# Channel attention and two feed-forward layers: a running account of engine time sets where weight and data operations stand

## The chip, the cores and the metric

The kernel runs on one core of a Trainium2 chip. The metric is the device time of one execution in microseconds (us). Below, PE is TensorE (matmuls; PEld is its weight load), ACT is ScalarE, DVE is VectorE, POOL is GpSimd and SP is SyncE, which here only issues DMAs.

## What is computed

```python
qn = q / (norm(q, axis=tokens) + 1e-6);  kn = k / (norm(k, axis=tokens) + 1e-6)
a = softmax(kn.T @ qn / tau)                  # 256 x 256, over 6080 tokens
x = v @ a                                     # 6080 x 256
x = square(relu(x @ w_in_1)) @ w_out_1        # 256 -> 2048 -> 256
h = x @ w_in_2                                # 256 -> 2048
y = (h * clip(h + 3, 0, 6) / 6) @ w_out_2     # 2048 -> 256
```

All inputs are float32 except the four weight matrices, which come as float64 words and are turned into float32 on the chip.

## The kernel before

**Steps.** After a head (scores, softmax, first weights) the program is a list of 96 steps, numbered i = 0 to 95 as in the code. There are two layers (`ph` 0 and 1), six chunks of tokens per layer (`c`), four blocks of 512 hidden columns (`u`) and two halves of such a block (`p`); a chunk is thus 8 steps. Every matmul product is made of three fp32r matmuls (high times high, high times low, low times high), and the 2 x 2 block products are done in seven multiplications, M1 to M7, instead of eight (Strassen's scheme in Winograd's form). A step (`step`, L764) runs the seven multiplications of its own hidden columns, 21 matmuls, and between them the 24 output matmuls of the step before, 45 in all. From step 8 on TensorE's order in a step is: M1, M2, M5, 3 output matmuls, M6, 5 outputs, M7, 6 outputs, M4, 5 outputs, M3, 5 outputs. So M6 is matmul 12 of the step, M7 matmul 20, M4 matmul 29 and M3 matmul 37, counted from 0.

**What TensorE waits for.** M1, M6, M7 and M4 share one PSUM tile `x`. After M1 ScalarE copies it out as `m1`, after M6 as `u2`, after M7 as `u3`, and after M4 it takes the activation of it (`act_psum`, tile `r`). M6 may start only when the copy `m1` has read the tile, M7 when `u2` has, M4 when `u3` has; M3 may start when VectorE has added `h22 = u3 + y`. VectorE makes the four sums h11, h22, h21 (here ScalarE and VectorE share), h12, and their activations (L806 in layer 0); ScalarE then rounds each to the high operand (`g<-h`), and VectorE subtracts to get the low operand (`g<-h,g`). What is left of h12 at the end of a step, its activation and its two operands, is done in the next step (`carry`).

**Background work.** The second layer's weights are prepared during the first layer's chunks 1 to 5, in tasks (`add_in_2`, `add_out_2`). For each `u` there are two conversions of `w_in_2` (`conv(0)`, `conv(1)`), each six operations: ScalarE `ct<-w` and `cv<-w`, then VectorE `ct<-ct` (L126), `ct<-ct` (L130), `ct<-ct,cv` (L142) and `wblk<-w,ct` (L134). A third task (`part`) takes from both conversions' blocks `wblk`: ScalarE rounds to a staging tile (`st<-wblk`, L108), VectorE subtracts (`st<-wblk,st`), SP stores both to DRAM. `w_out_2` goes the same way in two tasks (`convert_split`). Beside the tasks there is a `lane` of operations that split the next chunk's data (`b<-blk` on ScalarE; `blk<-blk` and `b<-blk,b` on VectorE). ScalarE, VectorE, SP, POOL and TensorE each work through their own queue in order; from step 8 on (`MANUAL_FROM = 8`, `phase[0] = 2`) these queues stand exactly in the order in which the source emits them.

**Where it is put.** `quota(i)` says how many background operations a step must take, `lane_quota(i)` the same for the lane. `beside(at)`, called at seven fixed places of the step, takes fixed shares of the two (`BESIDE_2`, `LANE`) and emits them there; an operation marked `waits` ends such a batch early.

```python
def beside(at):
    parts = BESIDE if i < MANUAL_FROM else BESIDE_2
    k = -(-todo[0] * parts[at] // max(1, sum(parts[at:])))
```

Of the kernel before, what the change touches and what calls it, by code (L numbers as in the profile page):

```python
# [62 lines left out]
def tile_channel_attention_then_two_ffn(  # L63
# [89 lines left out]

    def weight_sums(r):
        a21, a22, a11, a12 = (r[:, i] for i in range(4))
        return [
            lambda: add(a22, a21, a22),
            lambda: sub(a21, a11, a21),
            lambda: sub(a11, a22, a11),
            lambda: sub(a12, a12, a11),  # L160
        ]

    def data_prep(r, n, slots, new):


        b12, b22, b11, b21 = (r[:, i, :n] for i in range(4))
        of = {0: b22, 1: b11, 2: b21, "b12": b12, 3: b12, 4: b22, 5: b11, 6: b21}

        def one(slot):
            if slot == "sums":  # L170
                return [lambda: sub(b11, b12, b11), lambda: sub(b12, b22, b12),
                        lambda: sub(b22, b22, b11), lambda: sub(b21, b21, b22)]
# [5 lines left out]
            return [hi, lambda: sub(t[0][:, 1, :n], of[slot], t[0][:, 0, :n].bitcast(F32))]  # L178
        return [f for slot in slots for f in one(slot)]

    RAW, OTHER, SUMS = ((0, 3),), ((3, 4),), ((3, 5), (5, 7))
# [5 lines left out]
    def split_slots(r, ops, cuts):  # L187

        def one(a, b):
            parts = []  # L190

            def hi():
                parts.extend(t[:, a:b] for t in ops())
                return copy_act(parts[0], source(r, a, b))
            return [hi, lambda: sub(parts[1], source(r, a, b), parts[0].bitcast(F32))]
        return [f for cut in cuts for f in one(*cut)]

    def new_ops(pool, name):
# [13 lines left out]
    class Task:  # L212
        def __init__(self, name, load, due, alone, size):
            self.name, self.load, self.due, self.alone, self.size = name, load, due, alone, size
            self.steps, self.since = None, 0
# [18 lines left out]
    last_lo = [None, None, None]  # L234
    held, gate, marks = [], [], {}

    def waits(f):
        f.waits = True
        return f

    def background(n=1, calm=False):
        first = True
        while n > 0 and tasks:
            turn[0] ^= 1
# [3 lines left out]
            if calm and not first and getattr(t.steps[0], "waits", False):  # L248
                break
            first = False  # L250
            with ExitStack() as behind:
                for ins in gate if phase[0] == 1 else ():
                    behind.enter_context(tc.issue_after(ins))
                if t.name in held:
                    behind.enter_context(tc.issue_after(last_lo[2]))
                if phase[0] == 1:
                    for ins in marks.get(HELD_BEHIND.get(t.name), []) + marks.get("now", []):
                        behind.enter_context(tc.issue_after(ins))
                t.steps.pop(0)()
            n -= 1  # L260
            done[0] += 1
            if not t.steps:
                finished.add(tasks.pop(k).name)
                turn[0] = 0
                ensure_loads()
        return n

    def front(n, k=0):

# [33 lines left out]
    def out_cut(w, u, a):  # L303
        return w[u * 512 + a * P:u * 512 + (a + 2) * P]

    def convert_split(w, n, parts, done=None, fine=False, mark=True):

        def load():
            ws = words(w, n)
            got, x = [], []  # L310

            def make():
                steps, dst = from_f64_steps(None, ws, fine)
                x.append(dst)
                return steps

            def hi():
                got.extend(parts())
# [10 lines left out]
            return late(make, 6 if fine else 3) + [waits(hi), waits(lo)]  # L329
        return load  # L330

    def late(make, n):

        got = []

        def at(i):
# [4 lines left out]
            return waits(f) if i == n // 3 else f  # L341
        return [at(i) for i in range(n)]

    for u in range(NU):
        pool, tag = (gp, "g") if u == 0 else (oop, "oh")
# [6 lines left out]
    def add_w1(u, due=0, halves=(0, 1)):  # L352
        def conv(h):
            fine = u == 1 or (u, h) == (0, 1)

            def load():
                ws = words(in_cut(w_in_1, u, h), 1)
                return late(lambda: from_f64_steps(w1[u][:, h:h + 1], ws, fine)[0], 6 if fine else 3)
# [26 lines left out]
    def add_in_2(u, due):  # L385
# [3 lines left out]
        def conv(h):  # L389
            def load():  # L390
                ws = [x[:, 0].rearrange("p (g f) -> p g f", g=2) for x in words(in_cut(w_in_2, u, h), 1)]

                def make():
                    if not r:
                        r.append(blocks_tile("wblk"))
                    return from_f64_steps(r[0][:, h:4:2], ws, FINE)[0]
                return late(make, 6 if FINE else 3)
# [17 lines left out]
    def add_out_2(u, due):  # L415
        kept["o", u] = [dram.tile([P, 4, C], F32, tag="o2" + t, name="o2" + t, bufs=NU) for t in "hl"]
        for a in (0, 2):
            add_task(("o2", u) if a else None,
                     convert_split(out_cut(w_out_2, u, a), 2, lambda: staged(2),
                                   lambda st, a=a: keep([d[:, a:a + 2] for d in kept["o", u]], st), FINE), due)  # L420

    def fetch_2(nm, u):
        need((nm + "2", u))
# [279 lines left out]


    y_ps = {}

    def out_mms(ph, c, u, p, g):

# [24 lines left out]
    def y_done(ph, c, b, e, last=False):  # L733
# [15 lines left out]
        for k, (i, j) in enumerate(zip(cuts, cuts[1:])):  # L749
            if k:  # L750
                DVE.tensor_scalar(out=t[:, i:j], in0=y[:, i:j], scalar1=scale, scalar2=None, op0=ALU.mult)
            else:
                ACT.activation(out=t[:, i:j], in_=y[:, i:j], func=AF.Copy, scale=scale)
            (nc.gpsimd if ph == 0 else ACT if last and not k else SP).dma_start(out=dst[:, i:j], in_=t[:, i:j])

    def run_outs(outs, n):
        for _ in range(min(n, len(outs))):
            f, done = outs.pop(0)
            f()
            if done:  # L760
                y_done(*done)

    def step(i, ph, c, u, p, before, outs, carry):
# [2 lines left out]
        n = chunks[c][1]  # L766
        wh, wl = w_ops[ph, u]
        b_slots = b_ops[ph, c]
        todo = [quota(i) * (1 if i <= LAST else (0, 2)[i % (LAST + 1)] if i % (LAST + 1) < 2 else 1)]
        lane_todo = [lane_quota(i)]  # L770
        nxt_lane = bool(lane)

        def mul(dst, m, first):
# [2 lines left out]
            hi, lo = (b_slots[b][:, x, :n] for x in range(2))  # L776
            for k, (w, x) in enumerate(((wh, hi), (wh, lo), (wl, hi))):
                PE.matmul(dst, w[:, a, rows], x, start=first and k == 0, stop=k == 2, skip_group_check=True)  # L778

        def pop(k):  # L780
            run_outs(outs, k)

        def beside(at):
            parts = BESIDE if i < MANUAL_FROM else BESIDE_2
            k = -(-todo[0] * parts[at] // max(1, sum(parts[at:])))
            todo[0] -= k
            if k:
                todo[0] += background(k, phase[0] == 2)
# [58 lines left out]
        if plain:  # L847
# [27 lines left out]
            pop(len(outs))  # L875
            return g, (lambda: relu2(h12, x, 3), hi12, lo12)

        x = bank()[:, :n]
        mul(x, M1, True)
        marks["now"] = [copy_act(m1, x).ins]  # L880
        run(before)
        carry[0]()
        carry[1]()
        beside(0)
        pp = bank()[:, :n]
        mul(pp, M2, True)
# [1 line left out]
        carry[2]()  # L888
        y = bank()[:, :n]
        mul(y, M5, True)  # L890
        pops = AW_POPS if i == 0 else POPS if i < MANUAL_FROM else POPS_2
        pop(pops[0])
        act(h11, "1")
        beside(1)
# [163 lines left out]
```

## Time and profile before

| | us |
|---|---|
| time, median of 3 runs (lowest to highest) | 1072.03 (1071.76 to 1072.09) |
| the profiled execution, its own time | 1071.73 |
| its span, first to last instruction | 1069.9 |
| TensorE busy in the span | 1061.6 |
| VectorE, ScalarE, POOL busy | 896.7, 650.6, 22.5 |

The profiled execution has 1.8 us outside the span. Matmuls overlap in the records: one lasts some 0.39 us, but the next begins 0.23 us after it. A busy share of 99% therefore does not say that nothing is lost; the distance between the starts of neighbouring matmuls does.

### The profile page before, as it was taken

How to read it: one execution, taken by the hardware profiler on the slowest of the kernel's cores; microseconds unless marked ns; L12 is line 12 of the kernel's file. 1: busy time of each engine (PE TensorE's matmuls, PEld its weight loads, DVE VectorE, ACT ScalarE, POOL GpSimd, SP SyncE). 2: the span in 40 equal slices, each digit the busy share in tenths (PEclk: the TensorE clock that was granted, in tenths of full speed). 3: DMA queues.
4: the chain of work that ended last, by engine and by line, in shares of the span. 5: the costliest groups of instructions: out<-in, count | busy, mean ns of one | idle time of the engine just before them, and what ended most of it. 6: DMA issues, size and time to landing. Idle time of an engine off the chain costs nothing.

```text
span 1069.9 us, 12845 instructions
## 1 busy us (share of the span) xinstructions
PE 1061.6 (99%) x4602; PEld 865.6 (81%) x4602; DVE 896.7 (84%) x1520; ACT 650.6 (61%) x1129; POOL 22.5 (2%) x46
## 2 busy tenths in 40 slices
PE   9999999999999999999999999999999999999998
PEld 8778887888888888788888888888888888888886
DVE  6999888978878787887878988898898898898785
ACT  6698886566666667566565455455545555555443
POOL 0000000000000000001101000000000000000000
PEclk9999999999999999999999999999999999999999
DMA  9632230033123121314545002002002001001001
GB/s 359 246 99 91 67 118 20 30 121 95 40 95 102 50 68 69 108 46 174 181 152 185 1 1 78 1 1 78 1 1 78 1 1 59 20 0 39 1 1 39
DMA packets 31648, 78.03 MB, mean 73 GB/s; under 512 B 3296, under 2 KB 13792, under 8 KB 31584
## 3 DMA queue, kind: packets, MB, share of 16 engines
q1 hardware_dynamic: 27024, 57.49, 16.1%
q0 software_dynamic: 3840, 17.76, 4.8%
q10 hardware_dynamic: 720, 1.96, 0.5%
q8 instruction: 36, 0.59, 0.2%
q14 instruction: 28, 0.23, 0.1%
HBM read 53.22 MB, written 23.99 MB: 72 GB/s over the span
## 4 chain that ended last, share of the span: by engine, by line
PE 96%; DVE 2%; ACT 1%; DMA 0%; issue 0%; SPq 0%; ACTq 0%; DVEq 0%
PE y L720 48%; PE s L778 43%; PE sc L569 4%; PE s L499 1%; DMA w<-w_out_dram 0%; PE s L534 0%; DVE b L111 0%; ACT g L108 0%; DVE h L806 0%; DVE h L114 0%; DVE wl L111 0%; DVE g L111 0%; ACT ct L138 0%; ACT u L108 0%; DVE ct L142 0%
## 5 line engine op out<-in xcount | busy, mean ns | idle before, releaser
L720 PE MATMUL y<-g,oh 128*128 128x506 f32 (+1 forms) x1536 | 508.7, 392 | 0.0
L778 PE MATMUL s<-b,wh 128*128 128x506 f32 (+1 forms) x1356 | 422.4, 393 | 2.6 <-ACT u L108 1.9
L111 DVE TENSOR_TENSOR g<-h,g 128x506 fp32r<-128x506 f32 (+1 forms) x384 | 262.3, 683 | 99.4 <-ACT g L108 80.5
L720 PEld LDWEIGHTS y<-g,oh 128*128 128x128 f32 x1536 | 289.3, 188 | 64.4 <-DVE g L111 0.4
L778 PEld LDWEIGHTS s<-b,wh 128*128 128x128 f32 x1356 | 254.4, 188 | 63.7 <-ACT u L108 4.3
L720 PE MATMUL y<-g,ol 128*128 128x506 f32 (+1 forms) x768 | 302.0, 393 | 0.0
L778 PE MATMUL s<-b,wl 128*128 128x506 f32 (+1 forms) x678 | 266.0, 392 | 0.2 <-DVE wl L111 0.2
L108 ACT ACTIVATE g<-h 128x506 fp32r<-128x506 f32 (+1 forms) x384 | 235.3, 622 | 36.3 <-DVE h L827 14.2
L108 ACT ACTIVATE u<-s 128x506 f32<-128x506 f32 (+1 forms) x180 | 107.0, 595 | 141.7 <-PE s L778 140.7
L720 PEld LDWEIGHTS y<-g,ol 128*128 128x128 f32 x768 | 144.6, 188 | 31.8
L778 PEld LDWEIGHTS s<-b,wl 128*128 128x128 f32 x678 | 127.9, 189 | 29.0 <-DVE wl L111 1.1
L114 DVE TENSOR_TENSOR h<-u,s 128x506 f32<-128x506 f32 (+1 forms) x180 | 122.1, 678 | 27.2 <-ACT u L108 26.2
L108 ACT ACTIVATE m<-s 128x506 f32<-128x506 f32 (+1 forms) x90 | 53.6, 596 | 105.9 <-PE s L778 105.2
L810 DVE SCALAR_TENSOR_TENSOR h<-r,h 128x506 f32<-128x506 f32 (+1 forms) x144 | 98.9, 687 | 4.9
L806 DVE SCALAR_TENSOR_TENSOR h<-h 128x506 f32<-128x506 f32 (+1 forms) x121 | 82.6, 683 | 1.4
L826 ACT ACTIVATE r<-s,three 128x506 f32<-128x506 f32 (+1 forms) x48 | 32.9, 686 | 59.7 <-PE s L778 59.7
L114 DVE TENSOR_TENSOR h<-m,s 128x506 f32<-128x506 f32 (+1 forms) x90 | 61.2, 680 | 6.7 <-PE s L778 3.2
L809 DVE TENSOR_SCALAR r<-h 128x506 f32<-128x506 f32 (+1 forms) x144 | 60.6, 421 | 1.7
L111 DVE TENSOR_TENSOR b<-blk,b 128x506 fp32r<-128x506 f32 (+1 forms) x85 | 57.6, 680 | 0.9 <-ACT b L108 0.9
L108 ACT ACTIVATE b<-blk 128x506 fp32r<-128x506 f32 (+1 forms) x85 | 52.1, 616 | 0.2 <-DVE blk L111 0.2
L823 ACT ACTIVATE r<-s 128x506 f32<-128x506 f32 (+1 forms) x42 | 24.9, 594 | 32.5 <-PE s L778 30.0
L827 DVE SCALAR_TENSOR_TENSOR h<-r,s 128x506 f32<-128x506 f32 (+1 forms) x48 | 32.7, 681 | 9.7 <-ACT r L826 9.7
(97 smaller groups left out, 525.8 us busy)
## 6 DMA issues: line engine op xcount, KB each, us to landing
w<-w_in_dram SPq DMA_DIRECT2D x16, 512.0 KB, 4.6
w<-w_out_dram SPq DMA_DIRECT2D x16, 512.0 KB, 3.8
k<-k_dram SPq DMA_DIRECT2D x10, 512.0 KB, 7.0
blk<-vT_dram SPq DMA_DIRECT2D x8, 506.0 KB, 4.3
y<-y POOLq DMA_DIRECT2D x16, 253.0 KB, 2.5
blk<-y SPq DMA_DIRECT2D x8, 506.0 KB, 4.9
outT_dram<-y SPq DMA_DIRECT2D x15, 253.0 KB, 2.1
q<-q_dram SPq DMA_DIRECT2D x7, 512.0 KB, 7.7
```

Source lines behind the costliest of these rows:

```text
L108: return ACT.activation(out=out, in_=in_, func=AF.Copy)
L111: return DVE.tensor_tensor(out=out, in0=a, in1=b, op=ALU.subtract)
L114: return DVE.tensor_tensor(out=out, in0=a, in1=b, op=ALU.add)
L569: return lambda: PE.matmul(s_ps[dh][:, :C], t["k"][:, b, dh * P:(dh + 1) * P], t["q"][:, b], start=first, stop=last)
L720: PE.matmul(y_ps[ph, c, b, e][:, :n], w[:, j, e * P:(e + 1) * P], x, start=start, stop=stop)
L778: PE.matmul(dst, w[:, a, rows], x, start=first and k == 0, stop=k == 2, skip_group_check=True)
L806: DVE.scalar_tensor_tensor(out=h, in0=h, scalar=0.0, in1=h, op0=ALU.max, op1=ALU.mult)
L809: DVE.tensor_scalar(out=r, in0=h, scalar1=3.0, scalar2=0.0, op0=ALU.add, op1=ALU.max)
L810: DVE.scalar_tensor_tensor(out=h, in0=r, scalar=6.0, in1=h, op0=ALU.min, op1=ALU.mult)
L823: ACT.activation(out=r, in_=x, func=AF.Relu)
L826: ACT.activation(out=r, in_=x, func=AF.Relu, bias=three)
L827: DVE.scalar_tensor_tensor(out=h, in0=r, scalar=6.0, in1=x, op0=ALU.min, op1=ALU.mult)
```

## The change

The fixed shares go from step 8 on. In their place the source keeps a running account, in us, of when TensorE, ScalarE and VectorE will be done with what has been emitted so far (`now`). Each background operation carries its engine and a cost (`on`). Each emitted matmul adds 0.2305 to TensorE's account. At each place of the step `fill(act_until, dve_until)` emits, earliest start first, those background operations whose start plus cost, by the account, lies within the limit given for their engine. An operation marked `waits` may not start, by the account, before its task's `seen`: the end of the task's operation before it, or, for a task's first operation, the moment at which the task was loaded plus 3 us (`LANDING`). A task is loaded when it becomes one of the first two in the list; `part` loads nothing, and its `seen` is set in the same way.

The order of a step's own operations on each engine stays, and so does TensorE's whole order. Steps 0 to 7 are as before.

```diff
-BESIDE_2 = (1, 0, 2, 3, 2, 2, 2)
+MATMUL, SEEN, AFTER = 0.2305, 0.26, 0.12
+WIDE_ACT, WIDE_DVE, SCALAR_DVE, HALF_ACT, HALF_DVE = 0.55, 0.6, 0.46, 0.32, 0.31
+LANDING = 3.0
...
     def ensure_loads():
         for t in tasks[:2]:
             if t.steps is None:
-                t.steps, t.since = t.load(), done[0]
+                t.steps, t.since, t.seen = t.load(), done[0], now["PE"] + LANDING
...
+    now = {"PE": 0.0, "A": 0.0, "D": 0.0}
+    lane_seen, stagings = [0.0], [0.0, 0.0]
+
+    def on(engine, cost, f, waits=False, staging=0):
+        f.on, f.waits, f.staging = (engine, cost), waits, staging
         return f
+    def spend(engine, cost, ready=0.0):
+        now[engine] = max(now[engine], ready) + cost
+        return now[engine] + AFTER
+
+    def starts(f, seen):
+        ready = max(seen if f.waits else 0.0, stagings[-2] if f.staging == 1 else 0.0)
+        return max(now[f.on[0]], ready)
...
+    def emit(k):
+        t = tasks[k]
+        turn[0] = k
+        f = t.steps.pop(0)
+        f()
+        t.seen = spent(f, t.seen)
...
-            return [waits(hi) if a % 3 == 0 else hi, waits(lo)]
+            wide = b - a == 2
+            return [on("A", WIDE_ACT if wide else HALF_ACT, hi, True, 1), on("D", WIDE_DVE if wide else HALF_DVE, lo, True, 2)]
...
             f, done = outs.pop(0)
             f()
+            now["PE"] += MATMUL
...
-        todo = [quota(i) * (1 if i <= LAST else (0, 2)[i % (LAST + 1)] if i % (LAST + 1) < 2 else 1)]
+        todo = [quota(i)]
...
+        if phase[0] == 2:
...
+            def fill(act_until, dve_until):
+                until = {"A": act_until, "D": dve_until}
+                while True:
+                    fit = []
+                    if lane and lane_todo[0] > 0:
+                        fit.append((starts(lane[0], lane_seen[0]), -1, lane[0]))
+                    if todo[0] > 0:
+                        for k in choices():
+                            fit.append((starts(tasks[k].steps[0], tasks[k].seen), k, tasks[k].steps[0]))
+                    fit = [(start, k) for start, k, f in fit if start + f.on[1] <= until[f.on[0]]]
+                    if not fit:
+                        return
...
+            base = now["PE"]
+            squared = WIDE_DVE if ph == 0 else SCALAR_DVE + WIDE_DVE
+            x = bank()[:, :n]
+            mul(x, M1, True)
+            z12 = dve_op(carry[0], cost=carry_cost[0])
+            carry_cost[0] = squared
+            fill(seen() + 0.3, seen() + 1.2)
+            t = act_op(lambda: copy_act(m1, x), seen())
...
+            fill(base + 16 * MATMUL, t + 0.3)
+            dve_op(lambda: add(h11, m1, pp), t)
+            dve_op(carry[2], z12)
...
+            mul(x, M6, False)
+            fill(seen() + 0.1, base + 27 * MATMUL)
+            t = act_op(lambda: copy_act(u2, x), seen())
+            z11 = act_op(hi11, z11)
...
+            stand(t)
+            mul(x, M7, False)
```

**ScalarE in step 13.** `m`, then two `u`, then `r` are the copies after M1, M6, M7 and M4; before:

```order
L108 ACTIVATE u_1789<-s 128x508
L108 ACTIVATE st<-wblk 128x512
L823 ACTIVATE r<-s 128x508
L824 ACTIVATE h_1785<-r 128x508
L108 ACTIVATE g<-h_1786 128x508
L108 ACTIVATE g<-h_1785 128x508
L108 ACTIVATE m_1880<-s 128x508
L108 ACTIVATE g<-h_1784 128x508
L108 ACTIVATE st<-wblk 128x256
L108 ACTIVATE u_1881<-s 128x508
```

The same stretch, end of step 12 and beginning of step 13, now (line numbers are those of the changed kernel; its L112 is L108 of before):

```order
L112 ACTIVATE u_1784<-s 128x508
L869 ACTIVATE r<-s 128x508
L870 ACTIVATE h_1780<-r 128x508
L112 ACTIVATE g<-h_1781 128x508
L112 ACTIVATE g<-h_1780 128x508
L112 ACTIVATE m_1870<-s 128x508
L112 ACTIVATE g<-h_1779 128x508
L112 ACTIVATE b<-blk 128x506
L112 ACTIVATE st<-wblk 128x512
L112 ACTIVATE u_1871<-s 128x508
```

The first and wider staging copy of a `part` task stood behind the second `u` of step 12; it now stands ahead of the first `u` of step 13, behind `b<-blk`.

**VectorE in step 13**, from the activation of the last h12 on; before:

```order
L806 SCALAR_TENSOR_TENSOR h_1784<-h_1784 128x508
L114 TENSOR_TENSOR h_1876<-m_1880,s 128x508
L111 TENSOR_TENSOR g<-h_1784,g 128x508
L806 SCALAR_TENSOR_TENSOR h_1876<-h_1876 128x508
L111 TENSOR_TENSOR blk<-blk 128x506
L111 TENSOR_TENSOR st<-wblk,st 128x256
L111 TENSOR_TENSOR g<-h_1876,g 128x508
```

and now:

```order
L852 SCALAR_TENSOR_TENSOR h_1779<-h_1779 128x508
L115 TENSOR_TENSOR blk<-blk 128x506
L118 TENSOR_TENSOR h_1866<-m_1870,s 128x508
L115 TENSOR_TENSOR g<-h_1779,g 128x508
L852 SCALAR_TENSOR_TENSOR h_1866<-h_1866 128x508
L115 TENSOR_TENSOR b<-blk,b 128x506
L134 TENSOR_SCALAR ct<-ct 128x512
L146 ISA ct<-ct,cv 128x1024
L138 SCALAR_TENSOR_TENSOR wblk<-w_1641,ct 128x2x256
L115 TENSOR_TENSOR g<-h_1866,g 128x508
```

The conversion that writes the last part of `wblk` now ends in this step, ninth in the row shown. In step 30 the same two stretches read alike, with `b<-blk,b` in place of `blk<-blk` and one more `ct<-ct` in place of the second `b<-blk,b`, and no `b<-blk` ahead of `st<-wblk`.

**ScalarE at the start of step 8**, where `r<-h` and `h<-r` are the carried activation of step 7 (which ScalarE does up to that step); before:

```order
L108 ACTIVATE g<-h_1292 128x508
L108 ACTIVATE g<-h_1291 128x508
L108 ACTIVATE m_1411<-s 128x508
L803 ACTIVATE r<-h_1290 128x508
L804 ACTIVATE h_1290<-r 128x508
L108 ACTIVATE g<-h_1290 128x508
L108 ACTIVATE u_1412<-s 128x508
```

and now:

```order
L112 ACTIVATE g<-h_1292 128x508
L112 ACTIVATE g<-h_1291 128x508
L849 ACTIVATE r<-h_1290 128x508
L850 ACTIVATE h_1290<-r 128x508
L112 ACTIVATE wh<-wblk 128x512 x2
L112 ACTIVATE m_1411<-s 128x508
L112 ACTIVATE g<-h_1290 128x508
L112 ACTIVATE u_1412<-s 128x508
```

The copy `m` after M1 moved behind four operations: the carried activation and two weight copies `wh<-wblk`.

## Rows read from the trace of the kernel before

**Rows 1.** Page: busy us (share of the span) and instructions of each engine.

```profile
PE 1061.6 (99%) x4602; PEld 865.6 (81%) x4602; DVE 896.7 (84%) x1520; ACT 650.6 (61%) x1129; POOL 22.5 (2%) x46
```

**Rows 2.** Waits: who waited <- for whom: us in total, times, longest.

```profile
ACT ct L138 <- DMA w<-w_out_dram: 3.6, 1, 3.6
...
ACT st L108 <- DVE wblk L134: 3.0, 4, 0.8
```

**Rows 3.** Timeline, TensorE, steps 10, 36, 45: start, us, engine, instruction [idle <-releaser].

```profile
169.86 0.39 PE L720 MATMUL y<-g,ol 128*128 128x508 f32 x1
171.02 0.49 PE L778 MATMUL s<-b,wh 128*128 128x508 f32 x1 [0.78 <-ACT u L108]
...
440.61 0.39 PE L720 MATMUL y<-g,ol 128*128 128x506 f32 x1
442.11 0.73 PE L778 MATMUL s<-b,wh 128*128 128x506 f32 x2 [1.10 <-ACT u L108]
...
537.92 0.39 PE L720 MATMUL y<-g,ol 128*128 128x506 f32 x1
538.29 0.49 PE L778 MATMUL s<-b,wh 128*128 128x506 f32 x1
```

**Rows 4.** Timeline, TensorE, undisturbed step 24: its M1, its M7, the next M1.

```profile
311.78 0.62 PE L778 MATMUL s<-b,wh 128*128 128x506 f32 x2
...
316.38 0.61 PE L778 MATMUL s<-b,wh 128*128 128x506 f32 x2
...
322.13 0.39 PE L778 MATMUL s<-b,wh 128*128 128x506 f32 x1
```

**Rows 5.** Timeline, VectorE in the same step 24.

```profile
312.58 0.68 DVE L806 SCALAR_TENSOR_TENSOR h<-h 128x506 f32<-128x506 f32 x1
...
314.02 0.68 DVE L111 TENSOR_TENSOR g<-h,g 128x506 fp32r<-128x506 f32 x1
314.62 0.68 DVE L806 SCALAR_TENSOR_TENSOR h<-h 128x506 f32<-128x506 f32 x1
```

**Rows 6.** Timeline, ScalarE and VectorE, step 36: a copy, and a conversion's chain.

```profile
441.47 0.58 ACT L108 ACTIVATE u<-s 128x506 f32<-128x506 f32 x1
...
442.85 0.42 DVE L126 TENSOR_SCALAR ct<-ct 128x512 f32<-128x512 f32 x1
...
443.31 0.43 DVE L130 TENSOR_SCALAR ct<-ct 128x512 uint32<-128x512 uint32 x1
...
444.24 0.69 DVE L142 CUSTOM_DVE_ANT_0 ct<-ct,cv 128x1024 uint16<-128x1024 uint16 x1
...
444.96 0.69 DVE L134 SCALAR_TENSOR_TENSOR cv<-w,ct 128x512 uint32<-128x512 uint32 x1
...
445.69 0.63 ACT L108 ACTIVATE st<-cv 128x512 fp32r<-128x512 f32 x1 [2.00 <-DVE cv L134]
```

**Rows 7.** Timeline, TensorE (its M6), ScalarE and VectorE, start of step 8.

```profile
147.53 0.63 PE L778 MATMUL s<-b,wh 128*128 128x508 f32 x2
...
144.92 1.14 ACT L108 ACTIVATE g<-h 128x508 fp32r<-128x508 f32 x2
...
146.43 0.63 ACT L803 ACTIVATE r<-h 128x508 f32<-128x508 f32 x1
147.09 0.63 ACT L804 ACTIVATE h<-r 128x508 f32<-128x508 f32 x1
...
145.58 0.68 DVE L114 TENSOR_TENSOR h<-u,s 128x508 f32<-128x508 f32 x1
```

**Rows 8.** Timeline, TensorE: M1 of steps 76 and 77, undisturbed.

```profile
852.92 0.62 PE L778 MATMUL s<-b,wh 128*128 128x506 f32 x2
...
863.24 0.62 PE L778 MATMUL s<-b,wh 128*128 128x506 f32 x2
```

**Rows 9.** Windows: stretch, length, busy us (count) by engine, PEclk, DMA share, GB/s.

```profile
440.60:442.10 1.50, 0.41 (x2) 0.00 (x0) 1.40 (x3) 1.46 (x3) 0.00 (x0) 1.00 0.00 0
...
1065.00:1069.90 4.90, 0.46 (x2) 0.02 (x1) 0.42 (x1) 0.83 (x2) 0.00 (x0) 0.86 0.31 106
```

More of the change, by code (lines that the diff above doesn't have):

```diff
@@ L155, in weight_sums @@
         a21, a22, a11, a12 = (r[:, i] for i in range(4))
-        return [
+        return [on("D", HALF_DVE, f, not k) for k, f in enumerate((
             lambda: add(a22, a21, a22),
@@ L214, in __init__ @@
             self.name, self.load, self.due, self.alone, self.size = name, load, due, alone, size
-            self.steps, self.since = None, 0
+            self.steps, self.since, self.seen = None, 0, 0.0
     def ensure_loads():
@@ L235, in tile_channel_attention_then_two_ffn, with spent, choices, background @@
     held, gate, marks = [], [], {}
-    def waits(f):
-        f.waits = True
-        return f
-    def background(n=1, calm=False):
-        first = True
+    now = {"PE": 0.0, "A": 0.0, "D": 0.0}
+    lane_seen, stagings = [0.0], [0.0, 0.0]
+    def on(engine, cost, f, waits=False, staging=0):
+        f.on, f.waits, f.staging = (engine, cost), waits, staging
+        return f
+    def spend(engine, cost, ready=0.0):
[4 more added lines that the diff above has]
+        return max(now[f.on[0]], ready)
+    def spent(f, seen):
+        end = spend(*f.on, starts(f, seen))
+        if f.staging == 2:
+            stagings.append(end + LANDING)
+        return end
+    def choices():
+        if len(tasks) > 1 and not tasks[1].alone and done[0] - tasks[1].since > LOAD_AHEAD[2]:
+            return (0, 1) if turn[0] else (1, 0)
+        return (0,) if tasks else ()
+    def emit(k):
[4 more added lines that the diff above has]
+        t.seen = spent(f, t.seen)
+        done[0] += 1
+        if not t.steps:
+            finished.add(tasks.pop(k).name)
+            turn[0] = 0
+            ensure_loads()
+    def background(n=1):
         while n > 0 and tasks:
+            if phase[0] == 2:
+                emit(choices()[0])
+                n -= 1
+                continue
             turn[0] ^= 1
@@ L247, in background @@
             t = tasks[k]
-            if calm and not first and getattr(t.steps[0], "waits", False):
-                break
-            first = False
             with ExitStack() as behind:
@@ L328, in lo, with late @@
                     done(got)
-            return late(make, 6 if fine else 3) + [waits(hi), waits(lo)]
+            return late(make, fine) + [on("A", WIDE_ACT, hi, True, staging), on("D", WIDE_DVE, lo, True, 2 * staging)]
         return load
-    def late(make, n):
+    def late(make, fine):
         got = []
+        costs = [("A", WIDE_ACT)] * 2 + [("D", SCALAR_DVE)] * 2 + [("D", WIDE_DVE)] * 2
+        if not fine:
+            costs = [(e, 2 * cost) for e, cost in costs[::2]]
         def at(i):
@@ L340, in f @@
                 got[i]()
-            return waits(f) if i == n // 3 else f
-        return [at(i) for i in range(n)]
+            return on(*costs[i], f, i in (0, len(costs) // 3))
+        return [at(i) for i in range(len(costs))]
     for u in range(NU):
@@ L357, in load @@
                 ws = words(in_cut(w_in_1, u, h), 1)
-                return late(lambda: from_f64_steps(w1[u][:, h:h + 1], ws, fine)[0], 6 if fine else 3)
+                return late(lambda: from_f64_steps(w1[u][:, h:h + 1], ws, fine)[0], fine)
             return load
@@ L396, in make @@
                     return from_f64_steps(r[0][:, h:4:2], ws, FINE)[0]
-                return late(make, 6 if FINE else 3)
+                return late(make, FINE)
             return load
@@ L419, in add_out_2 @@
                      convert_split(out_cut(w_out_2, u, a), 2, lambda: staged(2),
-                                   lambda st, a=a: keep([d[:, a:a + 2] for d in kept["o", u]], st), FINE), due)
+                                   lambda st, a=a: keep([d[:, a:a + 2] for d in kept["o", u]], st), FINE, staging=1), due)
     def fetch_2(nm, u):
@@ L705, in tile_channel_attention_then_two_ffn @@
     y_ps = {}
+    carry_cost = [WIDE_DVE]
     def out_mms(ph, c, u, p, g):
@@ L778, in mul @@
                 PE.matmul(dst, w[:, a, rows], x, start=first and k == 0, stop=k == 2, skip_group_check=True)
+                now["PE"] += MATMUL
         def pop(k):
@@ L783, in beside @@
         def beside(at):
-            parts = BESIDE if i < MANUAL_FROM else BESIDE_2
-            k = -(-todo[0] * parts[at] // max(1, sum(parts[at:])))
+            k = -(-todo[0] * BESIDE[at] // max(1, sum(BESIDE[at:])))
             todo[0] -= k
-            if k:
-                todo[0] += background(k, phase[0] == 2)
+            background(k)
             k = min(len(lane), -(-lane_todo[0] * LANE[at] // max(1, sum(LANE[at:]))))
@@ L881, in step @@
         run(before)
-        carry[0]()
-        carry[1]()
+        run(carry[:2])
         beside(0)
@@ L890, in step @@
         mul(y, M5, True)
-        pops = AW_POPS if i == 0 else POPS if i < MANUAL_FROM else POPS_2
+        pops = POPS
         pop(pops[0])
```

83 lines of the change are left out of this document (76 added, 7 removed).

## The prediction, made before the changed kernel ran

> **What bounds the kernel now.** I read the page first. TensorE is busy 99% of the span, VectorE 84% and ScalarE 61% [rows 1], so a change of the order of ScalarE's and VectorE's work can only give back time in which TensorE stands still, or add such time. How much there is, the timeline of TensorE tells by the distance between starts: an undisturbed step has 45 matmuls in 10.35 us, 0.23 us each, and its M7 starts 4.60 us after its M1 [rows 4]. From step 8 on five distances stand out, all in front of M7, M4 or M3. The first is in step 10, 1.16 us; the largest in step 36, 1.50 us; the last in step 45, 0.37 us [rows 3]. The two between them, before M4 of step 29 and before M3 of step 36, I took out in the same way, 0.48 and 1.02 us. Less 0.23 us each they make 0.93 + 0.25 + 1.27 + 0.79 + 0.14 = 3.38 us. After a stall the next two matmuls are recorded with 0.73 us together, in an undisturbed step with 0.61 to 0.62 [rows 3, 4]: another 0.11 us each, 0.55 in all. **The ceiling of what the change can give back is thus about 3.9 us, 0.36%.**
>
> The releasers name the cause: the copy `u` came late [rows 3], since ScalarE works in order and a background operation stood ahead of it. In step 35 such an operation waited 3.6 us for a transfer of `w_out` [rows 2] and ScalarE was behind by that into step 36.
>
> **What the change takes away.** By the changed order no background operation stands ahead of `u` or of the second `u` with a wait at these five places: in steps 10 and 36 the first `u` has none between itself and the step's own copies, in 29 three whose operands have long been there, in 45 the one that stood before the second `u` is behind it. The first operation of each conversion now comes more than 9 us of matmuls after its load is emitted, so a wait like that of 3.6 us has no place. I take all 3.9 us as gone. Nothing is late next there: the step then runs at TensorE's own pace.
>
> **What the change adds.** Three places in the changed order have a `u` or `m` behind something that is not ready, because the account does not know of it. TensorE and all that ScalarE has behind the copy wait with it.
>
> *Step 13, M7.* The staging copy `st<-wblk` stands ahead of the first `u`. It needs the block `wblk` that the conversion's last VectorE operation writes; before, ScalarE's staging copies already waited for that operation, 3.0 us in 4 waits [rows 2]. For the account this copy is the first operation of a new task, bound only by the load time plus 3 us, not by the task before it, though `part` loads nothing and needs that one's result. When does the block come? In an undisturbed step VectorE takes up the carried activation 0.80 us after M1 (312.58 less 311.78) and then runs one operation in 0.60 us (314.02 to 314.62) [rows 4, 5]. In the changed order six such operations come first (carried activation, `blk`, `h` from `m`, low operand, activation, `b`): `ct<-ct` starts at 0.80 + 3.60 = 4.40. The next, dependent one follows 0.46 us later (442.85 to 443.31), at 4.86; `wblk` 0.72 us after that (444.24 to 444.96), at 5.58; the staging copy 0.73 us later (444.96 to 445.69), at 6.31 [rows 6]. ScalarE needs 0.52 us per copy (two in 1.14 us, one of them recorded with 0.62) [rows 7]: `u` at 6.83. From the start of a copy to the released matmul there are 0.64 us (441.47 to 442.11) [rows 3, 6]: M7 at 7.47 instead of 4.60. That is 2.87 us, with the slow restart **2.98**.
>
> *Step 30, M7.* The same copy, the next but one block. Five VectorE operations of 0.60 us come first, `ct<-ct` starts at 3.80, the second at 4.26, the third at 4.72, `wblk` at 5.44, the staging copy at 6.17, `u` at 6.69, M7 at 7.33: 2.73 us late, with the restart **2.84**. In steps 21 and 39, where the other two blocks are due, the copy stands behind both `u`, so that it holds only `r` and the rounding behind it.
>
> *Step 8, M6.* Here the account starts from zero and takes ScalarE and VectorE for idle; moreover it books the carried activation to VectorE, while in step 7 ScalarE does it, in two operations. `m` comes behind these and two weight copies. The sum h12 is added from 145.58 to 146.26 [rows 7]; ScalarE, which has been free since 145.96 (144.92 plus two times 0.52), starts the activation at 146.30, its second half 0.66 us later (146.43 to 147.09) at 146.96, the two weight copies at 147.48 and 148.00, `m` at 148.52, and M6 is released at 149.16. It ran at 147.53 [rows 7]: 1.63 us, with the restart **1.74**.
>
> *Steps 39 and 40.* In step 39 the staging copy, behind both `u`, gets its block late, since VectorE has three conversion operations and the data of the lane before it. By the same durations it starts 9.15 us into the step; `r` and the two roundings follow, VectorE gets the last low operands and h12 of the step some 2 us late, its carried activation starts 2.9 us into step 40, and the rounding for that, a narrow staging copy and `u` follow on ScalarE: M7 about 0.5 us late. This chain is long; its ends are 0, if it comes out 0.5 us shorter, and 0.9 us. I take **0.63** with the restart, as it comes out of the durations.
>
> Everything else that moves costs nothing by this reckoning: the lane's operations in steps 48 to 87 stand at a step's end or between the copies, where ScalarE idles; the DMAs that SP issues (loads, stores of staged weights) move with the operations in front of them, and the fetches that POOL issues in steps 41 to 48 stand behind the same matmuls as before. That cover is ScalarE's free time ahead of each `u`; the tightest fills (steps 29, 37, 41) leave 0.1 to 0.2 us of it, and would cost a few tenths together if it were gone.
>
> **The sum.** 2.98 + 2.84 + 1.74 + 0.63 = 8.19 us come, 3.9 us go: plus 4.3 us. On the profiled execution's own 1071.73 us that is 1076.0; the median of the runs lies 0.3 us higher, 1072.03, and gives **1076.3 us**, 0.4% slower. The unknown costs reach from 0 to 0.9 us at step 40 and some 0.3 us either way at each of the other three, and the pace of undisturbed steps differs too: 10.35 us in step 24, 10.32 in step 76 [rows 4, 8], at the same work. Which of these a step takes after a changed order, nothing in the profile tells; averaged over 11 chunks I allow 1 us either way.
>
> **The rivals.**
>
> 1. *The account holds, and the change does only what it is written for.* This is the other side: if the staging copies of steps 13 and 30 found their block ready and `m` of step 8 came in time, 1072.0 - 3.9 = 1068.1 us. It decides at one point, whether the last VectorE operation of the conversion ends before ScalarE reaches the copy. For it: in every other place the account's costs (0.55 and 0.6 us) are close to the 0.52 and 0.60 us of [rows 5, 7]. Against it: VectorE's order puts that operation ninth in the step, and ScalarE reaches the copy with nothing else to do some 2.7 us after M1. Chance 0.07.
>
> 2. *The pace.* Were all 88 steps to run at 10.32 instead of 10.35 us [rows 4, 8], 2.6 us would come back, and 1073.7 us would be no change that can be told. For it: both paces occur. Against it: one pace for all 88 steps does not occur before. Chance 0.07.
>
> 3. *The stalls cost more than their length.* TensorE's granted clock stayed at 1.00, the 2.4 GHz level, through the stall of 1.50 us; after its last matmul at 1065 it was granted 0.86 in the mean of the last 4.9 us [rows 9], so it did fall there towards 1.2 GHz once the engine had stood idle. Stalls of 2.9 us lie between the two. If the clock fell at both, and matmuls took twice 0.23 us for as long as the stall had lasted, some 6 matmuls would each lose 0.23 us, 1.4 us per stall: 1076.3 + 2.8 = 1079.1 us. The Trainium skill, page "TensorE: Matmul & The Clock Gate", Part 1, states the rule: the array's clock goes to half after the engine has been idle and comes back only after it has been busy again, so that by the page a long wait is paid a second time at its end. The trace bears the fall out at the program's end, and no stall before is long enough to show its price. A carry of the stalls into neighbouring steps (step 22 behind step 21 comes within 0.05 us of its limit) would end in the same region. Chance 0.10.
>
> **How the numbers follow.** The forecast has 0.76, the rivals 0.07, 0.07 and 0.10. The forecast's own spread is about 1074.4 to 1078.2. The range 1074.2 to 1078.5 holds nearly all of it and a part of the third rival, some 0.8. A measurement of this kernel can tell 0.2%, 2.1 us, from no change: faster means below 1069.9 (rival 1, 0.07), no change up to 1074.2 (rival 2, 0.07), slower the rest, 0.86.
>
> **What would show it.** In the profile of the changed kernel: TensorE's waits led by `s` behind ACT `u` and `m`, with single waits near 2.7, 2.6 and 1.5 us (the recorded idle time is 0.17 us shorter than the stall, 1.10 against 1.27 us in step 36); M7 of steps 13 and 30 some 7.4 us after their M1; ScalarE's `st<-wblk` waiting some 4 us for VectorE's `wblk` there; M6 of step 8 near 149.2 us; no distances over 0.3 us left in steps 10, 29, 36 and 45; clock 1.00 throughout. I am wrong if `u` of step 13 starts before 5 us of its step, if the five stalls of before stay, or if stalls come where I named none.

## The result, and the profile of the changed kernel

| | us |
|---|---|
| before, median of 6 runs (lowest to highest) | 1071.82 (1071.37 to 1072.09) |
| after, median of 6 runs (lowest to highest) | 1078.92 (1077.67 to 1079.68) |
| ratio, with its 95% interval | 1.0066 (1.0053 to 1.0079) |
| profiled execution of after, its span | 1078.93, 1077.1 |

The change costs 7.1 us, 0.7%. The direction, the places and the lengths of the stalls are those of the prediction, but it had 4.3 us, and the time lies 0.4 us above its range.

The page's row of busy times, which answers to [rows 1], hardly moved:

```profile
PE 1063.6 (99%) x4602; PEld 867.0 (80%) x4602; DVE 894.5 (83%) x1520; ACT 650.6 (60%) x1129; POOL 22.7 (2%) x46
```

TensorE is busy 2 us more with the same 4602 matmuls: some of them ran slower. The waits (who waited <- for whom: us in total, times, longest) show where TensorE stood still, and why; they answer to [rows 2]:

```profile
ACT st L112 <- DVE wblk L138: 13.1, 4, 4.0
...
PE s L825 <- ACT u L112: 5.6, 3, 2.7
...
PE s L825 <- ACT m L112: 1.5, 1, 1.5
...
ACT ct L142 <- DMA w<-w_out_dram: 0.3, 1, 0.3
```

ScalarE waits 13.1 us for `wblk` where it waited 3.0, and TensorE waits three times for a copy `u` and once for `m`. The wait of 3.6 us for a load of `w_out` is gone; the 0.3 us that are left stand at 80.45 us, ahead of step 8. The timeline (start, us, engine, instruction [idle <-releaser]) shows it in step 13, TensorE first, from M1 to the end of the slow matmuls:

```profile
198.12 0.62 PE L825 MATMUL s<-b,wh 128*128 128x508 f32 x2
...
202.49 0.39 PE L765 MATMUL y<-g,ol 128*128 128x508 f32 x1
205.57 1.03 PE L825 MATMUL s<-b,wh 128*128 128x508 f32 x2 [2.70 <-ACT u L112]
206.40 0.63 PE L825 MATMUL s<-b,wl 128*128 128x508 f32 x1
206.82 1.05 PE L765 MATMUL y<-g,oh 128*128 128x508 f32 x2
207.67 0.63 PE L765 MATMUL y<-g,ol 128*128 128x508 f32 x1
208.09 1.05 PE L765 MATMUL y<-g,oh 128*128 128x508 f32 x2
208.94 0.54 PE L765 MATMUL y<-g,ol 128*128 128x508 f32 x1
209.31 0.63 PE L825 MATMUL s<-b,wh 128*128 128x508 f32 x2
```

ScalarE and VectorE in the same step:

```profile
204.41 0.63 ACT L112 ACTIVATE st<-wblk 128x512 fp32r<-128x512 f32 x1 [3.62 <-DVE wblk L138]
204.95 0.58 ACT L112 ACTIVATE u<-s 128x508 f32<-128x508 f32 x1
...
202.51 0.42 DVE L134 TENSOR_SCALAR ct<-ct 128x512 uint32<-128x512 uint32 x1
...
203.69 0.69 DVE L138 SCALAR_TENSOR_TENSOR wblk<-w,ct 128x512 uint32<-128x512 uint32 x1
```

M7 runs 7.45 us after M1 instead of 4.60 [rows 4], released by `u`, which stands behind a staging copy, which waited for `wblk`. And after the stall, from 206.40 to 208.94, the matmuls follow each other at 0.42 us, not at 0.23. The windows (stretch, length, busy us by engine, PEclk, DMA share, GB/s) give the granted clock before, in and after the stalls of steps 13 and 30 and after that of step 8; they answer to [rows 9]:

```profile
202.50:205.80 3.30, 0.60 (x3) 0.23 (x2) 1.81 (x4) 1.39 (x3) 0.00 (x0) 1.00 0.00 0
205.83:209.25 3.42, 3.42 (x9) 2.67 (x9) 2.22 (x4) 0.80 (x2) 0.00 (x0) 0.50 0.20 77
209.25:213.00 3.75, 3.75 (x17) 3.03 (x17) 1.42 (x3) 2.75 (x6) 0.00 (x0) 1.00 0.19 70
383.24:386.70 3.46, 0.90 (x4) 0.47 (x3) 1.70 (x4) 1.62 (x3) 0.00 (x0) 1.00 0.06 22
386.74:390.15 3.41, 3.41 (x10) 2.68 (x9) 2.59 (x4) 0.59 (x1) 0.00 (x0) 0.50 0.14 52
...
149.01:153.00 3.99, 3.99 (x17) 3.30 (x18) 3.29 (x6) 2.85 (x6) 0.00 (x0) 1.00 0.57 215
```

Some 0.3 and 0.6 us after the end of the two long stalls the granted clock goes to 0.50, the 1.2 GHz level. It stays there for 3.4 us, though TensorE is busy all that time, and is back at 1.00 behind. In step 8 it stays at 1.00. The other stalls are these: M7 of step 30, M6 of step 8, and M7 of step 40, each behind the matmul ahead of it:

```profile
383.23 0.40 PE L765 MATMUL y<-g,ol 128*128 128x506 f32 x1
386.18 0.77 PE L825 MATMUL s<-b,wh 128*128 128x506 f32 x2 [2.56 <-ACT u L112]
...
147.16 0.40 PE L765 MATMUL y<-g,oh 128*128 128x508 f32 x1
149.01 0.72 PE L825 MATMUL s<-b,wh 128*128 128x508 f32 x2 [1.45 <-ACT m L112]
...
491.05 0.39 PE L765 MATMUL y<-g,ol 128*128 128x506 f32 x1
491.79 0.50 PE L825 MATMUL s<-b,wh 128*128 128x506 f32 x1 [0.35 <-ACT u L112]
```

The length of each step, M1 to the next M1, can be set against the same step in a kernel without any stall (e3_both, below). The steps of before that are longer than in that kernel (10, 18, 29, 36, 45) hold 3.95 us more; those of after (8, 13, 30, 40, 41) hold 1.71 + 4.54 + 4.40 + 0.62 + 0.08, with a few hundredths elsewhere 11.39 us. That is a difference of 7.4; the profiled executions differ by 7.2, since that of after reached step 8 0.14 us sooner.

### The profile page after: what moved, and what is told of

Read it like the earlier page. It is cut to its first block, busy times and chain, and to the rows that moved or that the text cites. A ratio compares the mean times of both kernels' runs of the same rounds, so it can differ in the third digit from the quotient of the medians.

```text
span 1077.1 us, 12850 instructions
## 1 busy us (share of the span) xinstructions
PE 1063.6 (99%) x4602; PEld 867.0 (80%) x4602; DVE 894.5 (83%) x1520; ACT 650.6 (60%) x1129; POOL 22.7 (2%) x46
## 4 chain that ended last, share of the span: by engine, by line
PE 94%; DVE 3%; ACT 1%; DMA 1%; issue 0%; ACTq 0%; DVEq 0%
PE y L765 48%; PE s L825 42%; PE sc L613 4%; DVE g L115 1%; DMA q<-q_dram 1%; DVE b L115 1%; PE s L543 1%; DVE h L118 0%; DVE h L852 0%; DVE ct L146 0%; ACT st L112 0%; ACT u L112 0%; DVE wblk L138 0%; DVE ct L134 0%; ACT wh L112 0%
## 5 line engine op out<-in xcount | busy, mean ns | idle before, releaser
L112 ACT ACTIVATE g<-h 128x506 fp32r<-128x506 f32 (+1 forms) x384 | 235.1, 622 | 26.1 <-DVE h L873 11.0
L112 ACT ACTIVATE u<-s 128x506 f32<-128x506 f32 (+1 forms) x180 | 107.0, 594 | 153.8 <-PE s L825 152.8
L112 ACT ACTIVATE m<-s 128x506 f32<-128x506 f32 (+1 forms) x90 | 53.3, 592 | 71.4 <-PE s L825 70.6
L112 ACT ACTIVATE b<-blk 128x506 fp32r<-128x506 f32 (+1 forms) x85 | 51.5, 616 | 14.8 <-PE s L825 14.6
```

The costliest lines, as they stand in the source:

```text
L112: return ACT.activation(out=out, in_=in_, func=AF.Copy)
```

## The experiments

All are built on the changed kernel.

**Is it one missing dependency?** Three theories at first: A, the account starts the staging copy of a task too early, since it does not know that `part` needs the task before it; B, the loads come later than 3 us, and so all conversions are late; C, the clock's cost comes from something else than the two long stalls, and stays when they go. The first kernel gives the account that one fact when a task ends:

```diff
             turn[0] = 0
             ensure_loads()
+            if tasks and tasks[0].name and tasks[0].name[0] == "w2":
+                tasks[0].seen = max(tasks[0].seen, t.seen)
```

> The changed kernel, with one thing told to the account: a `part` task may not start before the end of the task ahead of it. Theory A (the staging copy stands ahead of `u` because the account does not know that it needs the conversion's last VectorE operation; the long stalls cost once more through the clock): the stalls of steps 13, 30 and 40 go, which in the trace of the changed kernel make 4.54 + 4.40 + 0.61 us, and the clock stays at 1.00 to the end; step 8 keeps its 1.7 us. 1078.9 - 9.6 = 1069.3 us. Theory B (the loads land later than the 3 us that the account grants them, and ScalarE waits for those): nothing changes, 1078.9 us. Theory C (the clock's cost comes from something else than the two long stalls): the stalls go, some 6.3 us, but 3.1 us stay: 1072.5 us.

Measured: 1069.58 us (10 runs), ratio to before 0.9978 (0.9969 to 0.9987). Its waits of TensorE for ScalarE and of ScalarE for `wblk`:

```profile
PE s L827 <- ACT m L112: 1.5, 1, 1.5
...
ACT st L112 <- DVE wblk L138: 0.2, 1, 0.2
```

Of the 13.1 us for `wblk` 0.2 are left, and no wait of TensorE for `u`; the wait for `m` in step 8 stays. The granted clock is 1.00. Two lines are worth 9.3 us, more than the 7.1 that the change costs, and leave the kernel faster than before. This also takes the stall of step 40, which came from the staging copy in step 39. Theory A holds, and C, which had 1072.5 us, falls: what the clock cost went with the stalls.

The counter-test tells the account that the loads of the converting tasks take four times as long:

```diff
-                t.steps, t.since, t.seen = t.load(), done[0], now["PE"] + LANDING
+                t.steps, t.since, t.seen = t.load(), done[0], now["PE"] + (LANDING if t.name and t.name[0] == "w2" else 4 * LANDING)
```

> The changed kernel with four times the landing time (12 us) in the account for the tasks that really load; `part` is left as it is. Theory A: the staging copies of steps 13 and 30 still stand ahead of `u`, stalls and clock as in the changed kernel, 1078.9 us within 1.5 us. Theory B (loads land too late for the account): the long stalls go, about 1070 us.

Measured: 1078.87 us (2 runs), ratio 1.0062 (1.0044 to 1.0081). Of ScalarE's 1129 operations one changed its place (a `ct<-w` in step 38), and the row of waits is that of after, number for number. The stalls of steps 13 and 30 do not come from the landing time in the account, and B, which had about 1070 us, falls. That no load was late is shown by the trace of after itself: behind the 0.3 us at 80.45 us ScalarE waits for no load of weights.

```profile
ACT st L112 <- DVE wblk L138: 13.1, 4, 4.0
```

**Step 8 alone.** The account starts where ScalarE and VectorE stand at the end of step 7, the copy `m` goes ahead of the carried activation, and that is booked to ScalarE:

```diff
-            z12 = dve_op(carry[0], cost=carry_cost[0])
+            if i == MANUAL_FROM:
+                now["A"], now["D"] = base + 1.2, base + 2.6
+                t = act_op(lambda: copy_act(m1, x), seen())
+                z12 = act_op(carry[0], base + 1.6, 2)
+            else:
+                z12 = dve_op(carry[0], cost=carry_cost[0])
+                fill(seen() + 0.3, seen() + 1.2)
+                t = act_op(lambda: copy_act(m1, x), seen())
             carry_cost[0] = squared
-            fill(seen() + 0.3, seen() + 1.2)
-            t = act_op(lambda: copy_act(m1, x), seen())
```

> The changed kernel, with step 8 alone put right: the copy `m` ahead of the carried activation, and the account started from where ScalarE and VectorE are. Theory A: M6 of step 8 comes in time, 1.72 us less, all else as in the changed kernel, the clock too: 1077.2 us. If what ScalarE had to do ahead of `m` were not the cause, nothing would change: 1078.9 us.

Measured: 1077.75 us (4 runs), ratio 1.0048 (1.0034 to 1.0061). In step 8, `m` is now ready when TensorE needs it, and M6, 2.76 us after M1 at 145.03, has no wait (TensorE, then ScalarE):

```profile
147.56 0.40 PE L765 MATMUL y<-g,oh 128*128 128x508 f32 x1
147.79 0.62 PE L825 MATMUL s<-b,wh 128*128 128x508 f32 x2
...
146.22 0.58 ACT L112 ACTIVATE m<-s 128x508 f32<-128x508 f32 x1
146.70 0.63 ACT L849 ACTIVATE r<-h 128x508 f32<-128x508 f32 x1
```

The median lies 1.2 us below that of after, a little less than the 1.7 that step 8 lost; between e1_part_waits and the next kernel, where nothing falls in the clock, the same edit is worth 1.75.

**Both edits.**

> Both corrections together. Theory A: no stall from step 8 to the end, neither those of before nor the new ones: 1078.9 - 11.3 = 1067.6 us, which is also 1071.8 less the five stalls of before (3.9 us) within 0.4 us: faster than both kernels. If the placement by account has a cost of its own besides the named stalls, the time lies above that, at 1069 us or more.

Measured: 1067.83 us (5 runs), ratio 0.996 (0.9946 to 0.9973): faster than before by 0.4% and the fastest here. This is the prediction's first rival, 1068.1 us, made true by two corrections of the account. In its step 13 (M1 at 196.92) M7 comes after 4.60 us without a wait, and the staging copy now stands behind the second `u`, 0.21 us early (TensorE, then ScalarE):

```profile
201.52 0.61 PE L827 MATMUL s<-b,wh 128*128 128x508 f32 x2
...
200.56 0.60 ACT L112 ACTIVATE u<-s 128x508 f32<-128x508 f32 x1 [0.97 <-PE s L827]
...
203.21 0.63 ACT L112 ACTIVATE st<-wblk 128x512 fp32r<-128x512 f32 x1 [0.21 <-DVE wblk L138]
```

**What makes the clock fall, and what does a fall cost?** The stalls of steps 13 and 30 were as long as predicted, yet each step lost 1.56 us more. To see the price by itself I put stalls of chosen lengths into the kernel without any, in the second layer, where no weights are converted. The copies are extra work whose output nothing reads: `e` holds the softmax's numbers and is done with by then.

```diff
+            for _ in range({50: 5, 54: 7, 58: 8, 62: 9, 66: 10, 70: 11, 74: 12, 78: 13, 82: 15, 86: 18}.get(i, 0)):
+                copy_act(e_sb[0], e_sb[1])
             t = act_op(lambda: copy_act(u2, x), seen())
```

> The kernel of e3_both, with useless ScalarE copies (128x256, between two tiles no longer read) ahead of the copy u after M6 in ten steps of the second layer: 5, 7, 8, 9, 10, 11, 12, 13, 15, 18 copies in steps 50, 54, ..., 86. A 128x256 copy is recorded with 0.40 to 0.42 us, some 0.33 us apart if these overlap as the wider ones do, and ScalarE is free for 1.54 us ahead of u, so M7 should come 0.33 x copies - 1.54 us late: 0.1, 0.8, 1.1, 1.4, 1.8, 2.1, 2.4, 2.7, 3.4, 4.4, together 20.2 us, with slow restarts of 0.11 each 21.3. Theory A, the clock falls when one stall is long, whatever its cause: no granted clock under 1.00 after stalls up to 1.6 us (step 8 of the changed kernel), 0.50 after those from 2.7 us on (steps 13 and 30), the border somewhere between; five falls, give or take one, of 1.45 us beyond the 0.11: 1067.8 + 21.3 + 7.3 = 1096.4, and each fall costs the same whatever the stall's length. Rival F, the price grows with the stall (half of its length at every length): 1067.8 + 20.2 + 10.1 = 1098, with the largest extra, 2.2 us, in step 86. Rival G, the falls of steps 13 and 30 belong to what else runs there (conversions, transfers), not to the length: clock 1.00 in all ten steps, 1089.1.

> The same ten steps as in e5_lengths_up with the lengths the other way round: 18 copies in step 50, 5 in step 86. Theory A: the same time, 1096.4, and the same lengths with and without a fall, now in the other steps: falls in the first five or six of the ten. Rival F: 1098, the largest extra in step 50. Rival G: 1089.1. If the time since the program's start or the place in a chunk decided, the falls would stay in the same steps as in e5_lengths_up.

Measured: 1108.29 and 1107.82 us (one run each). The times are some 12 us above what I expected, first because the copies were mis-sized: they follow each other at some 0.45 us, not 0.33, and so made some 28 us of stalls instead of 20.2. (Each writes the tile of the one ahead, which may be why; no run tests it.) The rest is that the falls cost more than I had allowed. Eleven copies in e8_ten_of_2_5, below:

```profile
720.90 4.89 ACT L112 ACTIVATE e<-e 128x256 f32<-128x256 f32 x11
```

What counts is in the steps. The stall is the distance ahead of M7 less that of the undisturbed step; the extra is all that the step lost beyond it, slow restart and clock, read from TensorE's timelines of both kernels:

| copies | stall, us (up / down) | extra, us: up | extra, us: down |
|---|---|---|---|
| 5 | 0.16 / 0.21 | 0.12 | 0.10 |
| 7 | 1.12 / 1.12 | 0.10 | 0.10 |
| 8 | 1.58 / 1.66 | 0.09 | 0.13 |
| 9 | 2.02 / 2.03 | **1.63** | 0.10 |
| 10 | 2.46 / 2.47 | **1.62** | 0.13 |
| 11 | 2.93 / 2.91 | 0.13 | **1.53** |
| 12 | 3.38 / 3.37 | **1.67** | **2.82** |
| 13 | 3.82 / 3.81 | **2.72** | **1.66** |
| 15 | 4.70 / 4.69 | **2.27** | **2.15** |
| 18 | 6.05 / 5.99 | **1.45** | **2.59** |

The bold ones are the steps with matmuls at 0.42 us. The extra does not grow with the stall: it is 0.1 us without a fall, mostly 1.5 to 1.7 with one, and 2.2 to 2.8 in five steps. It goes by how long TensorE worked at the clock of 0.50. Two windows show this, the longest stall of e5_lengths_up (step 86) and a shorter one of e8_ten_of_2_5 (step 54):

```profile
992.25:999.05 6.80, 2.90 (x7) 2.35 (x8) 1.29 (x2) 4.74 (x11) 0.00 (x0) 0.50 0.00 0
```

```profile
632.33:639.15 6.82, 6.05 (x14) 4.80 (x15) 2.48 (x4) 2.39 (x5) 0.00 (x0) 0.50 0.00 0
```

The clock was at 0.50 equally long, but in the first TensorE stood still for most of that time and worked 2.90 us of it: 1.45 us extra, after a stall of 6.05 us. In the second it worked 6.05 us of it: 2.86 us extra, after a stall of 2.90. In the other falls of the table it worked 3.2 to 3.4 us (1.5 to 1.7 extra) or 4.5 to 6.0 us (2.2 to 2.8). So rival F falls, and G too, since the clock falls with no conversion near. The falls did not stay in the same steps either. But the length alone does not decide: at 2.0 and 2.5 us one order has a fall and the other none, and at 2.9 us it is the other way round. Theory A, that some border of length separates them, holds only below 1.7 and above 3.3 us.

**The same length ten times.** So I gave all ten steps the same number of copies, `if i in range(50, 90, 4): for _ in range(9)` (then 11, then 8). In the expectations I read the list above one copy off: nine make 2.0 us and eleven 2.9, not 1.6 and 2.5, and the last of the four puts this right.

> The kernel of e3_both with 9 useless copies ahead of u in all ten steps: ten stalls of 1.6 us (the length that 9 copies had in the two runs before, 1.58 and 1.66, both without a fall). Theory S, stalls up to this length leave the clock alone: 1067.8 + 10 x (1.62 + 0.10) = 1085.0, granted clock 1.00 after all ten, runs within 0.5 us of each other. Rival: at this length, too, the clock falls now and then: 1.45 us more for each, so 1086.5 and above, and runs apart by such steps.

> The same with 11 copies: ten stalls of 2.47 us, the length that fell in step 66 of one run before and not in step 70 of the other. Without a fall 1067.8 + 10 x (2.47 + 0.11) = 1093.6, and 1.5 us more for each fall. Theory M, the moment of the stall in the execution decides: some five of ten fall, about 1101, in other steps from one execution to the next, and runs apart by 1.5 us or multiples of it. Rival P, the step decides (what runs beside it, the order there): falls in the same steps in this run and the next, times within 0.5 us.

> The kernel of e8_ten_of_2_5 once more, for a second profile: theory M expects another set of steps with a fall and another number of them, rival P the same set.

> The same with 8 copies in all ten steps, which made 1.58 and 1.66 us in e5_lengths_up and e6_lengths_down (nine made 2.02, so the lengths named for the three runs before were each one copy short). Theory M with a shortest length: at 1.6 us no fall in any of the ten, 1067.8 + 10 x (1.62 + 0.10) = 1085.0, runs within 0.5 us of each other, clock 1.00. Rival: no shortest length, fewer falls only: at 2.0 us five of ten fell, so here some one to four, 1.5 us each, 1086.5 to 1091, and runs apart by such steps.

| kernel | stall | falls in ten | extra of a fall | runs, us |
|---|---|---|---|---|
| e10 (8 copies) | 1.5 to 1.6 us | 0 | | 1084.77, 1084.31, 1085.31 |
| e7 (9 copies) | 2.0 us | 5 | 1.65 to 1.68 | 1097.58, 1098.08 |
| e8 (11 copies) | 2.9 us | 5 | 1.52 to 1.67, one of 2.86 | 1106.49, 1098.24 |
| e9 (e8's kernel again) | 2.9 us | 1 | 1.66 | 1099.58, 1103.13 |

(The falls are those of the profiled execution, the first of its row.) The four runs of one and the same kernel in e8 and e9 lie 8 us apart, while the three of e10 keep within 1.0. Without a fall the kernel of e8 would take 1067.8 + 10 x (2.9 + 0.11) = 1097.9 us, which is nearly the lowest of its runs. The windows behind the stalls of steps 58, 62 and 70, first in e8, then in e9, show that the falls are not in the same steps:

```profile
680.40:683.40 3.00, 3.00 (x7) 2.46 (x8) 1.37 (x2) 1.04 (x2) 0.00 (x0) 0.50 0.02 5
726.35:729.35 3.00, 3.00 (x13) 2.48 (x14) 2.03 (x4) 1.03 (x2) 0.00 (x0) 1.00 0.00 0
816.75:819.75 3.00, 3.00 (x7) 2.46 (x8) 1.39 (x3) 1.02 (x2) 0.00 (x0) 0.50 0.00 0
```

```profile
677.90:680.90 3.00, 3.00 (x13) 2.48 (x14) 2.04 (x4) 1.01 (x2) 0.00 (x0) 1.00 0.03 5
...
811.25:814.25 3.00, 3.00 (x13) 2.50 (x14) 2.03 (x4) 1.02 (x2) 0.00 (x0) 1.00 0.00 0
```

In the same 3.0 us TensorE has 13 recorded matmuls at the full clock and 7 at half. The stalls ahead of the two windows of step 58 were alike (e8, then e9):

```profile
680.38 1.22 PE L827 MATMUL s<-b,wh 128*128 128x508 f32 x2 [2.75 <-ACT u L112]
```

```profile
677.85 0.73 PE L827 MATMUL s<-b,wh 128*128 128x508 f32 x2 [2.74 <-ACT u L112]
```

With the same instructions, the same step and the same length, one execution pays and the other does not. So rival P, the place in the program, falls. What decides differs from one execution to the next, as theory M has it; that it is the moment of the stall, no run shows by itself. For e10 the clock behind each of the ten stalls is full, and each step's extra is 0.08 to 0.12 us; here are the windows behind the first, the sixth and the last:

```profile
586.15:589.15 3.00, 3.00 (x13) 2.48 (x14) 2.02 (x4) 1.03 (x2) 0.00 (x0) 1.00 0.00 0
...
801.80:804.80 3.00, 3.00 (x13) 2.50 (x14) 2.01 (x4) 1.04 (x2) 0.00 (x0) 1.00 0.00 0
...
973.80:976.80 3.00, 3.00 (x13) 2.51 (x14) 2.04 (x4) 1.01 (x2) 0.00 (x0) 1.00 0.00 0
```

So a stall of step 8's length, 1.6 us, left the clock alone wherever it was seen, as theory S has it. What decides between 2.0 and 2.9 us was not settled. Nor was why both stalls of steps 13 and 30 fell in each of the three profiles that have them (after, e2_step8, e4_landing), while in the second layer 7 of 22 stalls of 2.9 us did. One of the six runs of after, 1077.67 us, has a mean granted clock of 0.998 against 0.996 in the others, and one of the four of e2_step8, 1075.91 us, 0.998 against 0.996 or 0.997; that would be one fall instead of two, but no profile of them shows it.

## Why the prediction was wrong, point by point

- **The stalls are right, instant by instant.** In step 13, counted from M1, I had `ct<-ct` at 4.40, `wblk` at 5.58, the staging copy at 6.31, `u` at 6.83 and M7 at 7.47; the rows above give 4.39, 5.57, 6.29, 6.83 and 7.45. In step 30 M7 is 2.72 us late (2.73), in step 40 0.51 (0.52), and M6 of step 8 comes 4.38 us after M1 (4.39). The slow restart of 0.11 us stands behind each stall at full clock. e1_part_waits and e2_step8 show the causes: the missing dependency of `part` on the task before it, and, in step 8, the account's false start with the carried activation booked to the wrong engine (one edit put both right).
- **What goes away is right.** 3.95 us against 3.9; none of the five stalls [rows 3] is left, and no new ones came where I named none (step 41 lost 0.08 us).
- **The pace, rival 2, did not move.** e3_both, with no stall and the same M1 to M1 distances of 10.30 to 10.43 us from step 8 on, still has both paces.
- **The step that failed is the clock.** I wrote "clock 1.00 throughout" into the forecast, and the fall into rival 3 with a chance of 0.10. Steps 13 and 30 lost 4.54 and 4.40 us where I had 2.98 and 2.84: 1.56 us each, 3.1 together, and that is the whole error of the account by steps (4.3 + 3.1 = 7.4). Between the medians it is 2.8 us (7.1 less 4.3). Rival 3 had the fall, and its 1.4 us per stall and 1079.1 us lie near what was measured, but the size was luck: it let the slow matmuls run for as long as the stall had lasted and lose 0.23 us each. In the runs the slow stretch does not go by the stall's length; here it was 3.4 us, some eight matmuls that lost 0.19 us each. And its chance was wrong. My only rows were a stall of 1.50 us that left the clock alone and an end of the program where it fell [rows 9], and 2.9 us lay between. I took the near end with nine chances in ten, where no row spoke for either. Of all profiled stalls of 2.7 to 2.9 us 13 of 28 fell: all six in steps 13 and 30, and 7 of the other 22. The rule that I cited from the Trainium skill, page "TensorE: Matmul & The Clock Gate", Part 1, is borne out by both stalls in that the clock went to half after idleness and came back only after work. With even half a chance per stall, the range had to reach to 1079.1 us and past it.
- **The range was therefore too narrow at the top**, by 0.4 us. It left most of rival 3 out although that was a known price with an unknown switch, and not a spread.

## What to carry to other kernels

A planner that keeps an account of time is only as good as its list of dependencies: one missing edge (a task that needs the result of the task before it) and one false start (step 8) turned a gain of 4.2 us into a loss of 7.1. In an engine that works in order, place no operation whose operand is still being made ahead of a copy that TensorE waits for, and follow each such copy back in both queues. And price a TensorE stall by its length only while rows show that the clock survives that length; beyond it, put the fall into the range as a switch, for each stall by itself.

## What the runs showed of the hardware that I had not expected

- A stall of 2.0 to 2.9 us may or may not drop the granted clock to 0.50: 6 of 12 at 2.0 us, 1 of 2 at 2.5, 13 of 28 at 2.7 to 2.9. None did up to 1.66 us (ten in e10, step 8's in three profiles, two in e5 and e6), all eight did from 3.37 us on.
- A fall has a price of its own, mostly 1.5 to 1.7 us with the restart, at times 2.2 to 2.9, and not by the length of the stall. TensorE runs at 0.42 instead of 0.23 us per matmul meanwhile, so that what counts is how long it works at the clock of 0.50: 2.9 us of it made 1.45 us, 6.05 us made 2.86. The fall may come a few matmuls after the work has begun again (in step 30 the first three matmuls still start at 386.18, 386.52 and 386.75).
- Small ScalarE copies (128x256) into one tile follow each other at some 0.45 us (eleven in 4.89 us), hardly faster than the 0.52 us of copies twice as wide that write different tiles [rows 7]. In step 40 of the changed kernel a copy into another tile began 0.31 us after such a small one (490.86 to 491.17).
